# Gate and value products of four more chunks by seven block products, and attention blocks transposed in one instruction and moved by DMA

## The chip, the core and the metric

The kernel runs on one core of a Trainium2 chip. A core has five engines that run side by side, each through its own list of instructions in order: TensorE (PE; its weight loads are listed apart as PEld), VectorE (DVE), ScalarE (ACT), GpSimd (POOL) and SyncE (SP), which issues nearly all DMA transfers here. Engines wait for each other by semaphores. The metric is device time in microseconds (us).

## The reference

```python
# attention: batch 8, heads 8, seq 576, head_dim 64, fp32
scores = scale * np.matmul(q, k.transpose(0, 1, 3, 2))
mask_local = (rel >= 0) & (rel < stride)                       # stride 32, heads 0 to 3
mask_strided = (rel >= 0) & (pos[None, :] % stride == pos[:, None] % stride)   # heads 4 to 7
attn = softmax(where(mask, scores, -1e9)); attn_out = attn @ v
# gated feed-forward over x = attn_out as [4608 tokens, 512]
rms = np.sqrt(np.mean(x * x, axis=-1, keepdims=True) + 1e-06)
xn = x / rms * rms_g
g = xn @ w_gate                                                # 512 -> 1536
silu = g * (1.0 / (1.0 + np.exp(-g)))
val = xn @ w_val
return (silu * val @ w_out).astype(np.float32)                 # 1536 -> 512
```

Both masks are sparse: only the score blocks that a mask leaves are computed.

## The kernel before, in words

**Attention.** Work is cut into 96 units `(b, p, j)`: a batch, a pair of heads, a third of the rows. A unit has two heads and one or two blocks of up to 128 query rows. `step_s` does scores (TensorE into the bank `pair`), row minimum with the mask (VectorE, L624, into `pp`), exponentials (ScalarE, L632) and normalisation (POOL or VectorE, L641). `step_t` transposes the probabilities into `pT`: since VectorE transposes blocks of 32 by 32, it issues one instruction for each 32-row block on the diagonal and beside it (L684). `step_o` multiplies by V and writes the result into `raw`, one buffer for each chunk of 512 tokens, three in turn. Units from 28 on (`BT`) have scores two at a time and values four at a time.

**Feed-forward.** There are 9 chunks of 512 tokens. In chunks 0 to 6 (`NCL` = 7) a slot is one of 12 units `u` of 128 hidden columns: gate product, value product (`gemm1`), gating (L922, L924, L935), and the output product (`slot_o`) of the slot before. Every fp32 product is made of three fp32r ones (high x high, low x high, high x low), so gate and value take 4 x 3 matmuls of 512 columns each and the output product 12. Chunks 7 and 8 are computed as a pair (`pair_of_chunks`): as a 2 x 2 block product (two chunks and two halves of the 512 inputs, times two halves and gate/value), by Strassen's scheme with seven block products of 6 matmuls per unit instead of eight. It uses four transformed weight blocks per unit, made by `transform_gv` during that stage, and for the output product `transform_o`, made beside earlier chunks.

**Buffers.** Gate and value weights of all 12 units stay in SBUF (`wg0` to `wv11`), split into high and low. Output weights pass through a ring of five buffers `or0` to `or4`: each slot reloads one from the copy `wos` in DRAM as soon as the slot five earlier has used it (`stream`, L1630).

**Order.** All work is entered as operations with a duration and the buffers that they read and write. A planner (`Plan`) puts them in order, engine by engine, by due times that it works out backwards; its switches (`PASS_A`, `PASS_B`, `SWITCH`, `BA`, `BM`) decide what goes first. At run time each engine keeps to its list.

Of the kernel before, what the change touches and what calls it, by code (L numbers as in the profile page):

```python
# [10 lines left out]
F32 = mybir.dt.float32  # L11
# [12 lines left out]
P = 128  # L24
# [4 lines left out]
NCL = NCH - 2  # L29
NX = 3  # L30
# [7 lines left out]
NCST = 510  # L38
# [19 lines left out]
BA = 10000.0  # L58
BM = 20000.0
# [42 lines left out]
NPB = 4  # L102
# [242 lines left out]
def attn_moe(ctx: ExitStack, tc: tile.TileContext, qT: bass.AP, kT: bass.AP, vl: bass.AP, vs: bass.AP,  # L345
# [13 lines left out]
    cb = sbt([P, 382], "cb", BF16)  # L359
    mloc = cb[:LQ, 0:256].rearrange("p (t k) -> p t k", k=P)  # L360
    m7 = cb[:126, 256:382]
    m6 = cb[:108, 256:364]
# [36 lines left out]
    identb = sbt([P, 2 * CH], "hl0", BF16)[:, 0:P]  # L399
    stat = [[sbt([P, 2, 2], f"mx{i}") for i in range(4)], [sbt([P, 2, 2, 2], f"su{i}") for i in range(4)]]  # L400
# [38 lines left out]
    for x in range(6):  # L439
        op("Pool", 100, -1, lambda x=x: nc.gpsimd.memset(xx[x][:, 0:PAD], 0.0), writes=[("xp", x)])  # L440
    for x in range(NPB):
        op("Pool", 600, -1, lambda x=x: nc.gpsimd.memset(pbuf[x], 0.0), writes=[("pp", x)])

    for i in range(4):
        op("Pool", 70, -1, lambda i=i: nc.gpsimd.memset(stat[1][i][:, :, :, 1:2], 1e-9), writes=[("st", i)])

# [3 lines left out]
    wus = [(b, p, j) for b in range(NB) for p in ((2, 3, 0, 1) if b == NB - 1 else range(NH // 2)) for j in range(3)]  # L450
# [4 lines left out]
    starts, turns, outs = {}, {}, {}  # L455
    for i in range(n_pro - TLAG, last + 1):
        s = i - n_pro
        if i >= n_pro:
            starts.setdefault(s - (i >= BT and (i - BT) % 2), []).append(i)
        if i < PP0:  # L460
            turns[s + TLAG] = turns.get(s + TLAG, []) + [i]
            d = s + TLAG + (i >= GR0 and (i - GR0) % 2 == 0 and i + 1 < PP0)
            outs[d] = outs.get(d, []) + [i]
        else:
            turns[s + 1] = turns.get(s + 1, []) + [i]
            d = s + (PG - 1 - (i - PP0) % PG if i < last - 3 else (last - i) % 2) + PVL
            outs[d] = outs.get(d, []) + [i]
# [6 lines left out]
    def tb(i):  # L474

        return (i - PP0) % PG if i >= PP0 else i % (NTB - 1)
# [18 lines left out]
    wos = [dp.tile([P, 1024], F32, name=f"wos{u}") for u in range(NU)]  # L495
    for n, u in keys:
        wraw[n, u] = sb.tile([P, 1024], U32, name=f"w{n}{u}")
# [12 lines left out]
    def slot_of(o, x):  # L510
        return (2 * o + x) % 6

    def load(b, p, at):
# [24 lines left out]
        if o == 0:  # L538
            op("SP", 430, at + 2, lambda: nc.sync.dma_start(out=identb, in_=consts[:, 382:510]), writes=[("hl", 0)],
               bytes_=P * P * 2)  # L540
            op("SP", 430, at + 2, lambda: nc.sync.dma_start(out=cb, in_=consts[:, 0:382]), writes=["cb"],
               bytes_=P * 382 * 2)
# [158 lines left out]
    def step_o(units):  # L701

        reads, length, todo = [], 0.0, []
        for x, i in enumerate(units):
# [4 lines left out]
            reads += [tk, ("vt", (4 * b + p) % 2)]  # L709
            length += 2 * len(tl) * 0.84 * m if i >= n_pro else PF * 2 * len(tl) * 1.26 * m + 30  # L710
# [14 lines left out]
        for x, (i, vt, m, n, tl, pT, po) in enumerate(todo):  # L725
            b, p, j = wus[i]
            base, nt = S * b, len(tl)
            cs = set()
# [23 lines left out]

            def evac(e, moves=moves):
# [39 lines left out]
    def rms(c, bk, at):  # L793
        if c == 1:
            op("PE", 900, at, lambda: nc.tensor.matmul(out=bank[bk], lhsT=ones, rhs=ssq, start=True, stop=True),
               reads=["ones", "ssq"], writes=[bk])
        elif c:
# [10 lines left out]
            def lo(e):  # L808
                two["l"] = sb.tile([P, CH], F32R, name="pT2")
# [6 lines left out]
            def blank():  # L816
                tbufs[2] = sb.tile([P, CH], F32, name="pT2")
                nc.gpsimd.memset(tbufs[2], 0.0)
            op("ACT", act(CH), at, hi, reads=["ssq"], writes=["srt"], also=[("DVE", 345, True)])
            op("Pool", pool(CH), at, lo, reads=["ssq", "srt"], writes=[("pT", 2)], also=[("DVE", dve(CH), True)])  # L820
            op("PE", 470, at, total, reads=["onesr", "srt", ("pT", 2)], writes=[bk] + ([("S", 0), ("T", 0)] if bk[0] == "b" else []))
            if c < NCL:
                op("Pool", 600, at, blank, writes=[("pT", 2)])
# [37 lines left out]
    def convert(c, at, kcs=range(KC)):  # L861
        rt = raw[c % NX]
        for kc in kcs:
# [90 lines left out]
    def slot_o(c, u, at):  # L954
        h = 0
        if (c, u) in ((1, 0), (1, 10), (2, 2), (3, 4), (4, 6), (5, 8)):
            b = plan.boost
            plan.boost = 0.0
            transform_o(u // 2, c)
            plan.boost = b  # L960
        for t in (0, 2, 1, 3) if c < NCL - 1 else range(4):
# [6 lines left out]
            op("PE", 681, at + t, fn, reads=[("hh", h), ("hl", h), wkey(("o", u, c))], writes=[("S", t // 2 + 1), ("T", t // 2 + 1), f"a{t}"] if u == 0 and c == 0 else [f"a{t}"], chain=True)  # L968
        stream(c, u)
        if u == NU - 1:  # L970
            for t in (0, 2, 1, 3):
                k, ob = (("ssq", ssq), ("srt", None), (("pp", 0), pbuf[0]), (("pp", 1), pbuf[1]))[t % 2]

                def evac(e, t=t, ob=ob):
                    ob = roots["srt"] if ob is None else ob
# [41 lines left out]
    def last_root():  # L1017
# [17 lines left out]
        def hi(e):  # L1035
            two["h"] = sb.tile([P, CH], F32R, name="pp0")
# [5 lines left out]
        def lo(e):  # L1042
            two["l"] = sb.tile([P, CH], F32R, name="pp1")
# [5 lines left out]
        op("ACT", act(CH), 0, hi, reads=[k0], writes=[("pp", 0)], also=[("DVE", 345, True)])  # L1049
        elementwise(CH, lo, [k0, ("pp", 0)], [("pp", 1)])  # L1050
# [48 lines left out]

    def transform_gv(u, z=0):  # L1100
# [676 lines left out]
```

## Time and profile before

| | |
|---|---|
| median of 3 runs | 1019.2 us (1018.59 to 1023.23) |
| profiled execution | 1019.23 us, its span 1017.4 us |
| granted TensorE clock, mean | 0.992 |
| matmul instructions in the trace | 5356 |
| HBM read, written | 98.09 MB, 22.02 MB |

The span runs from the first to the last instruction; the profiled execution's own time has 1.8 us around it. In the trace, chunk 0 runs from about 55 to 175 us, the pair at the end from about 835 us. "Busy" is the time in which an engine had an instruction under way. "Idle before" is the time just before an instruction, with the one that ended the wait.

### The profile page before, as it was taken

What the parts mean: (1) busy time and instruction counts of PE and PEld (TensorE: products, weight loads), DVE (VectorE), ACT (ScalarE), POOL (GpSimd) and SP (SyncE); (2) the same over time, 40 slices, a digit from 0 to 9 for tenths busy, and PEclk for the clock granted to TensorE, in tenths of its full rate; (3) what the DMA queues carried; (4) which work ended last, traced back from release to release, by engine and by line L of the source; (5) the groups of instructions that cost most, each with busy time, mean ns of one, the idle gap of its engine ahead of it and who ended that gap; (6) DMA issues with size and microseconds to landing.
All of it is one profiled execution on the core that took longest, in us unless ns stands there. A gap on an engine that the chain in (4) does not pass through costs nothing.

```text
span 1017.4 us, 15890 instructions
## 1 busy us (share of the span) xinstructions
PE 999.3 (98%) x5356; PEld 803.9 (79%) x5356; DVE 690.5 (68%) x1985; ACT 484.7 (48%) x1357; POOL 420.9 (41%) x400
## 2 busy tenths in 40 slices
PE   8999998999999999999999999999999999999998
PEld 6777775787887888788888888788877778887886
DVE  4699999715767617762566436777666968778891
ACT  6899966413454325441454226441554434334450
POOL 6333368414573313642236313263224443767500
PEclk9799999999999999999999999999999999999999
DMA  9876434423353214332243323232322101120451
GB/s 308 294 268 221 163 132 144 156 64 102 135 191 114 95 62 149 121 120 72 86 142 119 115 85 128 91 112 102 103 83 79 42 0 42 42 83 1 156 166 72
DMA packets 52561, 121.14 MB, mean 119 GB/s; under 512 B 5312, under 2 KB 21248, under 8 KB 52480
## 3 DMA queue, kind: packets, MB, share of 16 engines
q1 hardware_dynamic: 51712, 119.28, 35.1%
q10 hardware_dynamic: 768, 0.85, 0.3%
q8 instruction: 42, 0.69, 0.3%
q14 instruction: 39, 0.32, 0.1%
HBM read 98.09 MB, written 22.02 MB: 118 GB/s over the span
## 4 chain that ended last, share of the span: by engine, by line
PE 90%; DVE 7%; issue 1%; ACT 1%; DMA 1%; DVEq 0%; ACTq 0%
PE g L909 22%; PE v L909 21%; PE acc L966 21%; PE pair L604 4%; PE g L1295 3%; PE pair L721 3%; PE v L1295 3%; PE pair L1295 3%; PE g L1460 2%; PE acc L1460 2%; PE v L1460 2%; PE acc L1295 1%; PE pair L1460 1%; DVE pT L684 1%; DMA xx<-in_qT_dram 1%
## 5 line engine op out<-in xcount | busy, mean ns | idle before, releaser
L951 POOL TENSOR_TENSOR hl<-e,hh 128x512 fp32r<-128x512 f32 x84 | 115.1, 1370 | 271.9 <-ACT hh L942 260.4
L909 PE MATMUL g<-xh,wg 128*128 128x512 f32 x672 | 212.7, 398 | 1.0 <-DVE e L924 0.7
L966 PE MATMUL acc<-or,hh 128*128 128x512 f32 x672 | 210.1, 394 | 0.7 <-POOL or L1607 0.7
L909 PE MATMUL v<-xh,wv 128*128 128x512 f32 x664 | 208.6, 395 | 1.2 <-DVE wv L1607 0.9
L924 DVE SCALAR_TENSOR_TENSOR e<-e,g 128x512 f32<-128x512 f32 x84 | 57.5, 685 | 145.3 <-ACT e L922 144.8
L966 PEld LDWEIGHTS acc<-or,hh 128*128 128x128 f32 x672 | 124.7, 188 | 28.6 <-POOL or L1607 1.0
L909 PEld LDWEIGHTS g<-xh,wg 128*128 128x128 f32 x672 | 123.1, 188 | 30.3 <-DVE e L924 2.4
L909 PEld LDWEIGHTS v<-xh,wv 128*128 128x128 f32 x664 | 122.8, 188 | 30.2 <-DVE wv L1607 1.3
L909 PE MATMUL g<-xl,wg 128*128 128x512 f32 x336 | 131.3, 391 | 2.0 <-DVE xl L885 2.0
L966 PE MATMUL acc<-or,hl 128*128 128x512 f32 x336 | 131.0, 390 | 0.1
L641 POOL TENSOR_TENSOR pp<-pp,mx 96x512 f32<-96x512 f32 (+3 forms) x87 | 84.2, 975 | 109.7 <-DVE mx L638 64.7
L909 PE MATMUL v<-xl,wv 128*128 128x512 f32 x332 | 129.4, 390 | 0.0
L632 ACT ACTIVATE pp<-pp,mx 96x128 f32<-96x128 f32 (+2 forms) x296 | 113.5, 386 | 20.4 <-DVE mx L624 20.1
L942 ACT CAST hh<-e 128x512 fp32r<-128x512 f32 x84 | 52.2, 622 | 145.7 <-PE acc L966 131.9
L684 DVE STREAM_TRANSPOSE pT<-pp 32x128 f32<-32x128 f32 (+1 forms) x376 | 109.6, 292 | 14.5 <-POOL pp L641 7.7
L922 ACT ACTIVATE e<-g 128x512 f32<-128x512 f32 x84 | 50.1, 597 | 139.8 <-PE g L909 131.2
L935 DVE SCALAR_TENSOR_TENSOR e<-e,v 128x512 f32<-128x512 f32 x83 | 57.0, 687 | 32.2 <-PE v L909 27.2
L909 PEld LDWEIGHTS g<-xl,wg 128*128 128x128 f32 x336 | 63.2, 188 | 16.0 <-DVE xl L885 2.4
L966 PEld LDWEIGHTS acc<-or,hl 128*128 128x128 f32 x336 | 63.1, 188 | 14.2 <-POOL hl L951 0.7
L909 PEld LDWEIGHTS v<-xl,wv 128*128 128x128 f32 x332 | 62.3, 188 | 13.4
L624 DVE CUSTOM_DVE_ANT_0 pp<-pair,cb 96x128 f32<-96x128 f32 (+2 forms) x296 | 65.6, 277 | 10.2 <-PE pair L604 8.3
L632 ACT ACTIVATION_READ_ACCUMULATOR pp<-pp,mx 96x1 f32 (+2 forms) x296 | 55.8, 188 | 0.0
(494 smaller groups left out, 1620.4 us busy)
## 6 DMA issues: line engine op xcount, KB each, us to landing
or<-wos SPq DMA_DIRECT2D x72, 512.0 KB, 3.3
xx<-in_qT_dram SPq DMA_DIRECT2D x31, 288.0 KB, 3.4
xx<-in_kT_dram SPq DMA_DIRECT2D x28, 288.0 KB, 3.0
wg<-in_wgv_dram SPq DMA_DIRECT2D x12, 512.0 KB, 8.7
vt<-in_vl_dram SPq DMA_DIRECT2D x16, 384.0 KB, 3.7
wv<-in_wgv_dram SPq DMA_DIRECT2D x12, 512.0 KB, 6.0
or<-in_wo_dram SPq DMA_DIRECT2D x12, 512.0 KB, 3.6
wos<-or SPq DMA_DIRECT2D x12, 512.0 KB, 5.0
```

Source lines behind the costliest of these rows:

```text
L624: nc.vector.tensor_tensor_reduce(out=pv[:, h, x], in0=sp[h][:, x], in1=mk[:, x], scale=-0.125, scalar=3.0e38, op0=ALU.add, op1=ALU.min, ac ...
L632: nc.scalar.activation(out=pv[:, h, x], in_=sp[h][:, x] if i < PM else pv[:, h, x], func=AF.Exp, scale=0.125 if i < PM else -1.0, bias=mx[ ...
L641: (nc.vector if e == "DVE" else nc.gpsimd).tensor_tensor(out=pv, in0=pv, in1=mx.unsqueeze(3).broadcast_to([m, 2, nt, n]), op=ALU.mult)
L684: nc.vector.transpose(out=dst[32 * y:32 * y + 32, :, 32 * x:32 * x + 32], in_=src[32 * x:32 * x + 32, :, 32 * y:32 * y + 32])
L909: nc.tensor.matmul(out=out, lhsT=wt[:, w, sl], rhs=xhl[x, kc], start=(kc == 0 and i == 0), stop=(kc == KC - 1 and i == 2))
L924: op("DVE", dve(CH), at + MO, lambda: nc.vector.scalar_tensor_tensor(out=e, in0=e, scalar=1.0, in1=bank["g"], op0=ALU.add, op1=ALU.mult), ...
L935: op("DVE", dve(CH), at + MO, lambda: nc.vector.scalar_tensor_tensor(out=e, in0=e, scalar=0.5, in1=bank_of(c, ("v", u))[0], op0=ALU.mult, ...
L942: nc.scalar.copy(out=hh[h], in_=e)
L951: (nc.vector if n == "DVE" or h else nc.gpsimd).tensor_tensor(out=hl[h], in0=e, in1=hh[h].bitcast(F32), op=ALU.subtract)
L966: nc.tensor.matmul(out=acc[t], lhsT=x[h][:, sl], rhs=wt[:, w], start=(u == 0 and i == 0), stop=(u == NU - 1 and i == 2))
L1295: nc.tensor.matmul(out=banks[bk], lhsT=w, rhs=X[a, k].tile(y), start=start and k == 0 and i == 0, stop=stop and k == 1 and i == 2, skip_gr ...
L1460: nc.tensor.matmul(out=banks[bks[j]], lhsT=tile(v, k, j), rhs=x.tile(y), start=start and k == 0 and i == 0, stop=stop and k == KT - 1 and ...
```

## The change

Chunks 3 to 6 are now computed in two pairs as well, (3,4) and (5,6), by `plain_pair`: gate and value of the 12 units by seven block products each, all 24 gated tiles kept, and then the 24 output products as before, 12 matmuls each. To make room, the pair's split inputs lie in the places of the weights of units 0 to 4, and gated tiles in places of weights already used. So all gate and value weights are also written to DRAM once (`wgs`), the transformed weights too (`tgv`, made beside chunks 1 and 2), and they are loaded again when they are needed (`load_t`, `load_moved`, `back`). Attention units are spread over the slots so that both chunks of a pair are ready when it begins.

For units from 28 on, two units share one buffer of 1024 columns, laid out so that one VectorE instruction transposes all 32 x 32 blocks in place (`step_d`). The seven blocks on and beside the diagonal are then moved to other partitions by seven DMA transfers of 32 KB.

Other edits: `xx` has five buffers instead of six, `pp` and `pT` two of double width; `pT2` is no longer used for sums of squares; the planner's switches have other values.

```diff
+NS1 = 3
+MS = 6
+S0 = 13
-BA = 10000.0
-BM = 20000.0
+BA = 0.0
+BM = 0.0
-PASS_A = ([25.0, 0.0, 150.0, 37.5], 0.3, 4000.0, 8)
-PASS_B = ([25.0, 900.0, 225.0, 300.0], 0.2, 4000.0, 7)
-SWITCH = 180000.0
+PASS_A = ([50.0, 50.0, 300.0, 300.0], 0.1, 4000.0, 7)
+PASS_B = ([12.5, 450.0, 600.0, 800.0], 0.4, 4000.0, 3)
+SWITCH = 120000.0
...
+    def step_d(i):
+        x, u = (i - BT) // 2 % 2, (i - BT) % 2
...
+        op("DVE", DVT + 2 * CH / 0.96, 0, lambda: nc.vector.transpose(out=pq[x], in_=pq[x]), reads=[], writes=[("pu", x, 0), ("pu", x, 1), ("pp", x)])
+        moves = [(y, z) for y in range(4) for z in (y, y + 1) if z < 4]
+        for k, (y, z) in enumerate(moves):
+            op("SP", 430, 0, lambda y=y, z=z: nc.sync.dma_start(out=DX[x][32 * z:32 * z + 32, y].rearrange("k g q -> k (g q)"),
+                                                                in_=PX[x][32 * y:32 * y + 32, z].rearrange("k g q -> k (g q)")),
+               reads=[("pp", x)], writes=[("pd", x, k)], bytes_=32 * 1024)
...
+    def load_t(u, i):
+        for w in range(2):
+            def fn(w=w):
+                TS[i, w] = sb.tile([P, 2 * CH], F32R, name=f"{'tl' if w else 'th'}{i}" if i < 2 else f"or{w}")
+                nc.sync.dma_start(out=TS[i, w].bitcast(F32), in_=tgv[u][:, 1024 * w:1024 * w + 1024])
...
+    def plain_pair(c, beside):
...
+        natural = [f"w{n}{u}" for u in range(5) for n in "gv"]
...
+            args = {"1": ("A11", p, basic("g", 0), gk, True, False), "5": ("S1", r, trans(1), tkw, True, False),
+                    "6": ("S2", p, trans(2), tkw, False, False), "2": ("A12", q_, basic("g", 256), gk, True, True),
+                    "3": ("S4", r, basic("v", 256), vk, False, True), "7": ("S3", p, trans(3), tkw, False, False),
+                    "4": ("A22", p, trans(4), tkw, False, True)}
...
+        for u in range(RING):
+            ring_load(("o", u, c), every(wtag(("o", u, c)))[1:])
+        for tag in natural + ["wv8", "wv10"]:
+            back(tag)
...
+        for s in range(2):
+            for u in range(NU):
...
+                slot_o(c + s, u, 0, z, True)
...
+                if s == 1:
+                    back(hslot[u])
...
+        if n != "o":
+            op("SP", 430, at, lambda: nc.sync.dma_start(out=wgs[n, u], in_=W[key].rearrange("p w n -> p (w n)").bitcast(F32)),
+               reads=[wk], writes=[("wgs", key)], bytes_=P * 4096)
...
+    for c in range(NS1, NCL, 2):
+        plain_pair(c, beside)
     pair_of_chunks(NCL)
```

The change moves instructions at three places that matter below.

**TensorE, gate and value in chunk 3.** Before, unit 8: each row multiplies one of four input blocks (`xh` high, `xl` low) by the unit's gate (`wg8`) or value weights (`wv8`), into the bank `g` or `v`; x2 stands for two matmuls.

```order
L909 MATMUL g_68<-xh2_574,wg8_1324 128x512 x2
L909 MATMUL g_68<-xl2_579,wg8_1324 128x512
L909 MATMUL v_69<-xh2_574,wv8_1375 128x512 x2
L909 MATMUL v_69<-xl2_579,wv8_1375 128x512
L909 MATMUL g_68<-xh3_634,wg8_1324 128x512 x2
L909 MATMUL g_68<-xl3_666,wg8_1324 128x512
L909 MATMUL v_69<-xh3_634,wv8_1375 128x512 x2
L909 MATMUL v_69<-xl3_666,wv8_1375 128x512
```

Now one block product is six matmuls; the split inputs lie under the names of weights (`wg3`, `wv3`), the weights are transformed ones (`th0`, `tl0`) or reloaded ones (`wv7`, `wv8`), and the products go into four banks.

```order
L1820 MATMUL g_68<-wv3_3976,th0_4645 128x512
L1820 MATMUL acc01_70<-wg1_3449,wv7_4341 128x512 x3
L1820 MATMUL acc01_70<-wv1_3447,wv7_4341 128x512 x3
L1820 MATMUL acc23_71<-wg4_4053,wv8_4401 128x512 x3
L1820 MATMUL acc23_71<-wv4_4040,wv8_4401 128x512 x3
L1820 MATMUL g_68<-xh0_4020,th0_4645 128x512
```

The banks `acc01` and `acc23`, which the output product of the slot before filled between these rows, belong to gate and value here; the output products stand behind all twelve units.

**SyncE, reloads.** Before, in a chunk of the loop, output weights (`or` from `wos`) come one for each slot, among inputs of attention (`xx`, `vt`), transformed weights on their way out (`to`) and results.

```order
L1630 DMA or0_3655<-wos4_118 128x1024
L985 DMA out_0_dram<-srt_3490 128x512
L985 DMA out_0_dram<-ssq_100 128x512
L1630 DMA or1_3734<-wos5_119 128x1024
L554 DMA vt0_82<-in_vs_dram 126x2x320
L536 DMA xx0_76<-in_qT_dram 128x576
L536 DMA xx1_77<-in_kT_dram 128x576
L1630 DMA or2_3865<-wos6_120 128x1024
```

Now, where the output products of the pair (5,6) begin, gate and value weights (from `wsg`, `wsv`) stand between them; all but the `vt` row are 512 KB.

```order
L1925 DMA wg3_6811<-wsg3_132 128x1024
L1925 DMA wv2_6813<-wsv2_131 128x1024
L2085 DMA or0_6822<-wos5_119 128x1024
L1925 DMA wv3_6825<-wsv3_133 128x1024
L583 DMA vt1_82<-in_vl_dram 128x768
L1925 DMA wg4_6838<-wsg4_134 128x1024
L1925 DMA wv4_6841<-wsv4_135 128x1024
L1925 DMA wv10_6846<-wsv10_147 128x1024
L2085 DMA or1_6855<-wos6_120 128x1024
L2085 DMA or2_6871<-wos7_121 128x1024
```

The weight of slot 6 (`wos6`) moved behind four weights of the next stage in SyncE's queue.

**VectorE and SyncE, the transposes.** Before, VectorE's list beside a late chunk has the block transposes of two units as seven instructions each (x4 and x3, for the two halves of a unit's blocks).

```order
L935 SCALAR_TENSOR_TENSOR e_99<-e_99,v_69 128x512
L684 STREAM_TRANSPOSE pT1_97<-pp1_93 32x4x32 x4
L684 STREAM_TRANSPOSE pT0_96<-pp0_92 32x4x32 x3
L684 STREAM_TRANSPOSE pT1_97<-pp1_93 32x4x32 x3
L810 TENSOR_TENSOR pT2_6014<-ssq_100,srt_6002 128x512
```

Now VectorE has one row for two units, `STREAM_TRANSPOSE pp1_92<-pp1_92 128x1024`, and SyncE seven moves behind it; here with what each waits for (DMAHW0 to 7 are eight counters that transfers take in turn, so a wait on one is for the transfer eight places earlier).

```order
L1226 DMA tg6_156<-th0_2004 128x1024 [waits DMAHW4_49,Activation_49]
L1226 DMA tg6_156<-tl0_2058 128x1024 [waits DMAHW5_49,DVE_49]
L663 DMA pT1_94<-pp1_92 32x256 [waits DMAHW6_49,DVE_49]
L663 DMA pT1_94<-pp1_92 32x256 [waits DMAHW7_49]
L663 DMA pT1_94<-pp1_92 32x256 [waits DMAHW0_49]
L663 DMA pT1_94<-pp1_92 32x256 [waits DMAHW1_49]
L663 DMA pT1_94<-pp1_92 32x256 [waits DMAHW2_49]
L663 DMA pT1_94<-pp1_92 32x256 [waits DMAHW3_49]
L663 DMA pT1_94<-pp1_92 32x256 [waits DMAHW4_49]
L2085 DMA or4_3250<-wos5_119 128x1024 [waits DMAHW5_49,DVE_49,PE_49]
```

The values product of TensorE waits for the last of the moves instead of the last block transpose.

More of the change, by code (lines that the diff above doesn't have):

```diff
@@ L455, in attn_moe @@
     starts, turns, outs = {}, {}, {}
+    where = {}
+    for i in range(n_pro - TLAG, BT):
+        where[i] = i - n_pro
+    i0, s0 = BT, S0
+    for c in range(NS1, NCL + 1, 2):
+        i1 = min(12 * (c + 2), last + 1)
+        for i in range(i0, i1):
+            where[i] = s0 + int((i - (i - BT) % 2 - i0) * (NU * c - (MS if c < NCL else MSL) - s0) / (i1 - i0))
+        i0, s0 = i1, NU * c + 1
     for i in range(n_pro - TLAG, last + 1):
-        s = i - n_pro
+        s = where[i]
         if i >= n_pro:
-            starts.setdefault(s - (i >= BT and (i - BT) % 2), []).append(i)
+            starts.setdefault(s, []).append(i)
         if i < PP0:
@@ L474, in tb @@
     def tb(i):
-        return (i - PP0) % PG if i >= PP0 else i % (NTB - 1)
+        return (i - BT) // 2 % 2 if i >= BT else i % (NTB - 1)
     def tkey(i):
@@ L495, in attn_moe @@
     wos = [dp.tile([P, 1024], F32, name=f"wos{u}") for u in range(NU)]
+    wgs = {(n, u): dp.tile([P, 1024], F32, name=f"ws{n}{u}") for n, u in keys}
+    tgv = [dp.tile([P, 2048], F32, name=f"tg{u}") for u in range(NU)]
+    done_x, done_u = set(), set()
     for n, u in keys:
@@ L510, in slot_of @@
     def slot_of(o, x):
-        return (2 * o + x) % 6
+        return (2 * o + x) % (5 if o < XO else 4)
     def load(b, p, at):
@@ L751, in step_o @@
                     i1 = i2
+            assert all(c < NX or c - NX in done_x for c in cs), (i, cs)
             def evac(e, moves=moves):
@@ L793, in rms @@
     def rms(c, bk, at):
+        busy.discard(c)
+        rooted.add(c)
+        assert not flight or c < 2
+        assert all(i in done_u for i in range(12 * (c + 1) - 4 * (c == NB - 1))), c
         if c == 1:
@@ L952, in slot_h, with slot_o @@
         op("Pool", pool(CH), at + MO, lo, reads=[ek, ("hh", h)], writes=[("hl", h)] + more, also=way("f", ("DVE", dve(CH), True)))
[L954 to L961, printed above, removed]
+    def slot_o(c, u, at, h=0, far=False):
+        first = c >= NS1 and (c - NS1) % 2 == 0 and u == 0
+        for t in (0, 2, 1, 3):
             def fn(t=t):
@@ L1365, in quad @@
             return step, after
-        transform_gv(2, 0)
+        for u in range(NS):
+            load_t(u, u)
         steps = [quad(u) for u in range(NU)]
@@ new lines, in scores_of @@
+    def scores_of(units):
+        for i in units:
+            b, p, j = wus[i]
+            if j == 0:
+                load(b, p, 0)
+                if i < PP0:
+                    load_v(b, p, 0)
+        if units[0] >= BT:
+            todo = [step_e(i) for i in units]
+            op("PE", SC0 + sum(x[2] for x in todo), 0, lambda: [x[0]() for x in todo], reads=[y for x in todo for y in x[1]],
+               writes=[("S", 0), ("T", 0)], lock=("b0", "b1"))
+            for x in todo:
+                x[3]()
+            return
+        for i in units:
+            step_s(i)
@@ new lines, in values_of, with before @@
+    def values_of(units):
+        step_o(units)
+        for i in units:
+            b, p, j = wus[i]
+            if j == (2 if b < NB - 1 or p > 1 else 0):
+                square(b, p, 0)
+            n = turn.index((b, p)) + 2
+            if j == 2 and i + 4 >= PP0 and n < len(turn):
+                load_v(*turn[n], 0)
+    def before(s):
+        plan.boost = BA if s >= NU * CB else 0.0
+        for i in turns.get(s, []):
+            if i < PP0:
+                step_t(i)
+        if s in starts:
+            scores_of(starts[s])
@@ new lines, in behind, with roots_of, beside @@
+    def behind(s):
+        plan.boost = BA if s >= NU * CB else 0.0
+        if s in outs:
+            values_of(outs[s])
+        for i in turns.get(s, []):
+            if i >= PP0:
+                step_t(i)
+    def roots_of(s, bk="g"):
+        for c in range(1, NB - 1):
+            if not flight and c not in rooted and all(i in done_u for i in range(12 * (c + 1))):
+                rms(c, bk, 0)
+    def beside(s):
+        before(s)
+        behind(s)
+    tslots = {TV0 + k * (NU * NS1 - 2 - TV0) // NU: k for k in range(NU)}
@@ L1681, in attn_moe @@
+    for c in range(NS1):
+        more = c + 1 < NS1
+        for u in range(NU):
+            at, s = T(c, u), NU * c + u
+            before(s)
             plan.boost = BM if c >= CB else 0.0
@@ L1685, in attn_moe @@
                 convert(c + 1, at + CVO)
-            plan.boost = BA if c >= CB else 0.0
-            if pvs:
-                values_of(pvs)
-            for i in turn:
-                if i >= PP0:
-                    step_t(i)
+            now = u == 0 and c > 0 and not flight
+            if now:
+                plan.boost = BM if c >= CB else 0.0
+                slot_o(c - 1, NU - 1, at + SOO)
+            behind(s)
             plan.boost = BM if c >= CB else 0.0
```

556 lines of the change are left out of this document (436 added, 120 removed), and 2 rows, old and new, of the table xplace.

## The prediction

> **What bounds the kernel now.** I read the page first: the busy line, the chain of work that ended last, the rows on DMA. The first says who is busy, the second who is late, the third what is left of a resource that the change uses more.
>
> ```profile
> PE 999.3 (98%) x5356; PEld 803.9 (79%) x5356; DVE 690.5 (68%) x1985; ACT 484.7 (48%) x1357; POOL 420.9 (41%) x400
> ...
> DMA  9876434423353214332243323232322101120451
> GB/s 308 294 268 221 163 132 144 156 64 102 135 191 114 95 62 149 121 120 72 86 142 119 115 85 128 91 112 102 103 83 79 42 0 42 42 83 1 156 166 72
> ...
> q1 hardware_dynamic: 51712, 119.28, 35.1%
> ...
> PE 90%; DVE 7%; issue 1%; ACT 1%; DMA 1%; DVEq 0%; ACTq 0%
> ```
>
> TensorE is busy for 98% of the span and holds 90% of the chain. So a matmul that goes is worth its own time, as long as nothing else becomes late. DMA is used to 35%: 119.28 MB took 35.1% of 16 engines over 1017.4 us, which makes 334 GB/s at full use; the busiest slice reached 308.
>
> Then I asked for busy times by stage: PE, PEld, DVE, ACT, POOL, granted clock, DMA share and GB/s in each stretch.
>
> ```profile
> 55.00:175.00 120.00, 114.29 (x640) 87.53 (x640) 113.63 (x291) 99.80 (x248) 60.01 (x47) 1.00 0.53 182
> 175.00:295.00 120.00, 119.99 (x636) 96.88 (x637) 70.94 (x261) 51.04 (x151) 53.83 (x51) 1.00 0.37 123
> ...
> 835.00:960.00 125.00, 123.22 (x543) 101.53 (x542) 101.12 (x138) 51.94 (x90) 76.92 (x64) 1.00 0.19 60
> ...
> 800.00:825.00 25.00, 24.16 (x105) 19.03 (x103) 20.18 (x23) 8.48 (x14) 15.51 (x10) 1.00 0.07 22
> 850.00:875.00 25.00, 25.00 (x112) 20.69 (x111) 20.01 (x28) 9.61 (x17) 14.20 (x13) 1.00 0.01 3
> 925.00:950.00 25.00, 23.21 (x103) 18.86 (x102) 21.66 (x27) 9.82 (x17) 16.30 (x13) 1.00 0.09 27
> ```
>
> Chunk 1 on (175 us) leaves TensorE without a gap and VectorE 59% busy. Chunk 0 (55 to 175 us) is the warning: with VectorE at 113.63 of 120 us, TensorE lost 5.71 us. In the pair at the end (835 to 960 us), VectorE at 101.12 of 125 cost TensorE 1.78 us.
>
> **The change part by part.** All of it is set against the profiled execution, 1019.23 us (span 1017.4 and 1.8 around it), which equals the median of the runs shown, 1019.2.
>
> *Fewer products.* A pair of chunks needs 12 x 2 x 24 = 576 matmuls of 512 columns for gate and value; by seven block products it needs 12 x 7 x 6 = 504. Two pairs save 144. At 25.00/112 = 0.223 us (row of 850 us) that is **-32.1 us**, all on the path.
>
> *Wider attention blocks.* Score blocks of 108 columns become 128, and so do the transposed ones.
>
> ```profile
> L604 PE MATMUL pair<-xx,xx 64*108 64x108 f32 x168 | 13.0, 271 | 0.0
> ...
> L604 PE MATMUL pair<-xx,xx 64*126 64x126 f32 x112 | 9.4, 285 | 0.0
> ...
> L721 PE MATMUL pair<-pT,vt 108*64 108x108 f32 x108 | 8.0, 263 | 0.2 <-DVE pT L684 0.2
> ```
>
> The program has 72 such score and 72 such value matmuls after unit 28; the trace records each as two. 13.0/168 = 77 ns against 9.4/112 = 84 ns: 7 ns for 18 columns more, 144 records, 1 us, and less for the values. In proportion to the columns (18%) it would be 2 us each. I take **+2 us** (1 to 4).
>
> *Transposes.* 444 block transposes go; 34 instructions of 1024 columns come.
>
> ```profile
> L684 DVE STREAM_TRANSPOSE pT<-pp 32x128 f32<-32x128 f32 x320 | 96.4, 301 | 13.2 <-POOL pp L641 7.2 <-PE pair L721 1.6
> ...
> L684 DVE STREAM_TRANSPOSE pT<-pp 32x64 f32<-32x64 f32 x56 | 13.2, 236 | 1.3 <-POOL pp L641 0.5
> ```
>
> 64 columns more cost 65 ns, so 1024 columns are about 1.2 us: 41 us for what took some 130. This relief lies off the path, so I count it only in VectorE's load below.
>
> *VectorE in chunks 1 and 2.* Here the change piles work up: the attention of chunks up to 4 must be ready when chunk 3 begins, so 120 row minima instead of 72 run beside these slots, and all twelve gate/value transforms with six output transforms. From the second chunk's first gating multiply to the third chunk's last the order gives VectorE:
>
> ```profile
> L624 DVE CUSTOM_DVE_ANT_0 pp<-pair,cb 96x128 f32<-96x128 f32 x156 | 35.3, 281 | 0.7 <-POOL pp L641 0.4
> ...
> L924 DVE SCALAR_TENSOR_TENSOR e<-e,g 128x512 f32<-128x512 f32 x84 | 57.5, 685 | 145.3 <-ACT e L922 144.8
> ...
> L853 DVE RECIPROCAL srt<-srt 128x128 f32<-128x128 f32 x28 | 24.1, 911 | 0.0
> ...
> L1094 DVE TENSOR_TENSOR tl<-tt,th 128x512 fp32r<-128x512 f32 x9 | 9.6, 1066 | 0.3
> ...
> L1015 DVE TENSOR_TENSOR tt<-tt 128x256 f32<-128x256 f32 x13 | 7.1, 572 | 0.3
> ...
> L1011 DVE TENSOR_TENSOR tt<-wv 128x512 f32<-128x512 f32 x6 | 6.3, 1050 | 0.0
> ...
> L1011 DVE TENSOR_TENSOR tt<-wg 128x512 f32<-128x512 f32 x4 | 2.7, 681 | 0.0
> ```
>
> 120 row minima at 35.3/156 = 0.226 (27 us), 16 large transposes (19), 46 gating multiplies at 0.685 (32), 12 reciprocals and 12 scalings at about 0.91 (22), 19 sums at 0.68 to 1.05 (13 to 20), 43 half differences at 0.572 (25), 29 low parts at 0.68 to 1.07 (20 to 31), and some 42 us of copies, casts, reductions and small sums: **200 to 218 us**. TensorE has 23 slots x 36 x 0.223 = 185 us there and some 30 of attention, 215 us. So VectorE stands at 93% or more, as in chunk 0, where TensorE lost 5.71 of 120. In proportion that is 10 us; where the short durations hold, 2 us as in the pair stage. I take **+7 us** (-2, since chunk 0 itself loses six transposes, to +34).
>
> *DMA in the output stages.* Per pair, gate and value use up the buffers in which weights stood. So 24 output products of 12 x 0.223 = 2.68 us each follow one another, and beside them the weights come back. Program order from the first reload of the second pair's end to its last output weight has 46 transfers of 512 KB, and with outputs and moves 26.5 MB; in the first pair 23.3 MB. TensorE's counted work from their first chance to the last need is about 76 and 74 us. At 334 GB/s the transfers take 79 and 70 us. The tight place is slot 6 of the second: 10.8 MB are queued ahead of its weight and its two neighbours, 32 us at 334, with about 26 to spare. I take **+6 us** (0, if the first are issued early enough, to 12 at 308).
>
> [...] The trace here never shows more than 308 in a slice.
>
> *Block moves.* Seven transfers of 32 KB follow each transpose.
>
> ```profile
> SPq L1567 <- DMA wos<-or: 19.5, 7, 3.9
> ...
> 39.17 0.33 SPq L551 DMA_DIRECT2D vt<-in_vl_dram  x1
> ...
> wg<-in_kT_dram ACTq DMA_DIRECT2D x1, 48.0 KB, 2.3
> or<-wos SPq DMA_DIRECT2D x72, 512.0 KB, 3.3
> ...
> L632 ACT ACTIVATE pp<-pp,mx 96x128 f32<-96x128 f32 x156 | 60.6, 391 | 8.7 <-DVE mx L624 8.6
> ...
> L632 ACT ACTIVATION_READ_ACCUMULATOR pp<-pp,mx 96x1 f32 x156 | 29.4, 188 | 0.0
> ...
> L641 POOL TENSOR_TENSOR pp<-pp,mx 96x512 f32<-96x512 f32 x42 | 45.9, 1100 | 55.7 <-DVE mx L638 50.4 <-DVE mx L637 2.7 <-DVE v L830 2.4
> ```
>
> An issue holds SyncE's queue 0.33 us or more, a landing takes 2.3 to 3.3: 5 to 6 us from the transpose to the values, where a transposed block was usable at once. Also each issue waits until the eighth transfer before it has landed (the order shows the counters; the first row above is such waits). The cover: row minima 2, exponentials 8 x (60.6 + 29.4)/156 = 4.6, normalisation 1 to 2, transpose 1.2 and moves 5 to 6 make 14 to 16 us after a pair's scores, and TensorE's order puts 16.6 to 45 us of its own work between the second scores of a group and its values. Behind a late values product stand the gate products of the next slot. Four of the 17 groups have under 18 us. I take **+2 us** (0 to 34).
>
> *Epilogues beside attention.* The seven-product stage ran without attention so far and lost 1.78 of 125 us; now ScalarE's blocks of exponentials (half of those 4.6 us a unit) stand between its copies. Two such stages: **+3 us** (0 to 10). In return the gaps of the last pair, 0.84 and 1.79 us at 800 and 925 us, end beside transforms that are done by then: **-2 us**.
>
> Sum: -32.1 + 2 + 7 + 6 + 2 + 3 - 2 = **-14 us, 1005 us**.
>
> **The rivals.**
>
> *Nothing is late.* For it: TensorE stood 0.01 us in 120 from 175 us on, though seven chunks of dependent work ran beside it. Against it: the 5.71 us of chunk 0 at the same load of VectorE. 1019.2 - 32.1 + 2 + 1 = 990 us.
>
> *DMA becomes the bound of the output stages.* All traffic grows from 119 to 220 MB. At the 308 GB/s of the busiest slice the second stage stalls 12 us, the first 4, and reloads run over into the next gate products: some 16 instead of 6, 1015 us. For it: 26.5 MB in 76 us is 349 GB/s. Against: the rate of 334 is measured over small transfers too.
>
> *VectorE takes TensorE's place in chunks 1 and 2.* This one ends slower. The forecast gains 21 us without its +7, so it decides from the point where VectorE needs 236 us there, 224 us of work at 95%. The longest rows show how:
>
> ```profile
> L1094 DVE TENSOR_TENSOR or<-xx,or 128x512 fp32r<-128x512 f32 x2 | 3.4, 1718 | 0.0
> ...
> L885 DVE TENSOR_TENSOR xl<-raw,xh 128x512 fp32r<-128x512 f32 x17 | 15.1, 891 | 0.0
> ```
>
> With 29 low parts at 1.72 and the sums at 1.05 it is 237 us, at 95% use 249, 34 us over TensorE's 215: 1032 us. Against it: 1.72 is a mean of two.
>
> *The moves come late.* If each of the 17 groups holds TensorE 2 us, that is 34 instead of 2: 1037 us; from 1 us a group the gain is gone. For it: a move stands behind 512 KB transfers in one queue. Against: the slack above.
>
> [...]
>
> That the change doesn't do what it says is left at 1 in 50: the order counts 144 matmuls fewer.
>
> **How the numbers follow.** The forecast (997 to 1013) gets 0.42, nothing late 0.17, DMA 0.15, VectorE 0.13, late moves 0.10, the rest 0.03. The likeliest gives 1005 us. The range 989 to 1026 leaves out most of the two slow cases and little below. A measurement of this kernel can tell about 0.5%, 5 us. Faster (under 1014): forecast, nothing late, two thirds of DMA: 0.68. Within 0.5%: the rest of DMA and the mild ends of the slow cases, 0.14. Slower: 0.18.
>
> **What would show it.** Right: about 3650 matmuls of 512 columns at 0.22 us; PE gaps in chunks 1 and 2 of some 7 us with VectorE over 90%; gaps in the output stages released by a DMA into the output weights' ring; large transposes of about 1.2 us. Wrong: PE waits on the moves' landing summing to over 10 us, output stages without gaps at over 330 GB/s, or VectorE under 85% in chunks 1 and 2 with gaps nonetheless.

## The result and the profile after

| | before | after |
|---|---|---|
| median (range) | 1019.25 us (1018.59 to 1023.23, 4 runs) | 1030.42 us (1029.04 to 1033.63, 4 runs) |
| profiled execution, its span | 1019.23 us, 1017.4 us | 1029.79 us, 1026.9 us |
| granted TensorE clock, mean | 0.992 | 0.988 |
| matmul instructions in the trace | 5356 | 5212 |

The ratio is 1.0106, 95% interval 1.0071 to 1.0141: the changed kernel is slower by about 11 us, where 14 less were forecast.

The page of the changed kernel, with the lines that answer to those of before (busy time by engine, DMA share and GB/s in 40 slices, the queue that carries nearly all transfers, the chain that ended last):

```profile
PE 987.6 (96%) x5212; PEld 780.4 (76%) x5212; DVE 743.1 (72%) x1749; ACT 501.5 (49%) x1394; POOL 302.1 (29%) x286
...
DMA  9999654456467476355666869554679793462551
GB/s 301 314 377 354 220 207 167 145 192 226 157 210 273 138 235 227 122 168 199 198 204 211 292 231 369 204 199 162 192 235 355 241 391 117 151 205 82 155 174 61
...
q1 hardware_dynamic: 88768, 220.43, 62.8%
...
PE 76%; DVE 10%; DMA 8%; SPq 2%; ACT 2%; issue 1%; POOL 0%; ACTq 0%; DVEq 0%
```

144 matmuls are gone, but TensorE's busy time fell by 11.7 us (999.3 to 987.6), not by 32. And its idle time rose from 18.1 to 39.3 us (span less busy). These are two separate losses. The chain shows the second: DVE, DMA and SP's queue hold 20% of it now.

Where the idle time lies is told by busy times in stretches (columns as before: PE, PEld, DVE, ACT, POOL, granted clock, DMA share, GB/s):

```profile
55.00:175.00 120.00, 113.41 (x607) 85.99 (x607) 112.83 (x269) 96.10 (x241) 45.98 (x38) 0.99 0.74 274
175.00:295.00 120.00, 113.84 (x663) 88.13 (x664) 100.00 (x286) 61.96 (x207) 70.58 (x62) 1.00 0.52 171
295.00:400.00 105.00, 94.21 (x579) 74.11 (x577) 85.22 (x223) 54.30 (x168) 63.15 (x55) 0.97 0.66 220
...
325.00:350.00 25.00, 18.78 (x109) 15.13 (x109) 20.80 (x62) 13.94 (x43) 16.33 (x15) 0.86 0.46 143
...
825.00:850.00 25.00, 24.65 (x118) 19.63 (x115) 22.10 (x37) 6.27 (x13) 0.00 (x0) 1.00 1.02 403
...
875.00:900.00 25.00, 25.00 (x110) 20.34 (x110) 12.12 (x19) 7.52 (x13) 0.00 (x0) 1.00 0.41 137
```

In chunks 1 and 2 (175 to 400 us) TensorE idles 225 - 208.05 = 17 us, in stretches that had no gap before. VectorE is not full there: 100.00 of 120 and 85.22 of 105 us, 83 and 81%. The row of 875 us shows the first loss: TensorE without a gap, products of 512 columns only, 110 in 25 us where before had 112.

Groups of instructions (busy, mean ns of one, idle before and its releasers):

```profile
L616 DVE CUSTOM_DVE_ANT_0 pp<-pair,cb 96x128 f32<-96x128 f32 (+2 forms) x248 | 55.5, 283 | 27.9 <-DMA pT<-pp 15.8 <-PE pair L610 8.6 <-PE acc L1088 2.9
L660 DVE STREAM_TRANSPOSE pp<-pp 128x1024 f32<-128x1024 f32 x34 | 42.1, 1237 | 9.1 <-POOL pp L646 8.9
```

VectorE's row minima (L616) waited 15.8 us for the block moves. One such place, in order of time (start, duration, engine, line, operation; idle before in brackets):

```profile
319.22 2.12 SPq L583 DMA_DIRECT2D vt<-in_vl_dram  x2
...
319.34 1.22 DVE L660 STREAM_TRANSPOSE pp<-pp 128x1024 f32<-128x1024 f32 x1
...
321.44 4.36 SPq L663 DMA_DIRECT2D pT<-pp  x7
...
327.83 0.29 DVE L616 CUSTOM_DVE_ANT_0 pp<-pair,cb 96x128 f32<-96x128 f32 x1 [0.93 <-DMA pT<-pp]
...
329.65 0.58 PE L610 MATMUL pair<-xx,xx 64*126 64x128 f32 x2 [4.57 <-DVE my L616]
```

The transpose ends at 320.56. SP is still issuing two other loads, then the seven moves, 0.62 us each, until 325.80; the last lands about 2 us later. Only then may a row minimum write into that buffer again, and VectorE keeps to its order. The next scores wait for those row minima to empty the bank `pair`: TensorE stands for 4.57 us. The granted clock of 325 to 350 us, 0.86, shows what came with this gap: half the clock from 327.4 to 334.2 us, and so for 4.5 us after TensorE had begun again at 329.65. In this trace shorter gaps were followed by it, too: after 2.46 us at 149 us and after 2.29 us at 782 us the clock was halved for 3.4 us each, while in run e9 (below) one of 2.5 us before 175 us passed without (granted clock 1.00 over 55 to 175 us, 0.99 here).

An account of the 9.5 us between the two spans: 144 products fewer at 227.6 ns, -32.8; idle time, +21.2; clock not granted (1.2% of 1026.9 against 0.8% of 1017.4 us), +4; slower products, +12.7 (next section); wider blocks +2; some 2 us remain unexplained.

### The profile page after: what moved, and what is told of

Read it like the earlier page. It is cut to its first block, busy times and chain, and to the rows that moved or that the text cites. A ratio compares the mean times of both kernels' runs of the same rounds, so it can differ in the third digit from the quotient of the medians.

```text
span 1026.9 us, 16263 instructions
## 1 busy us (share of the span) xinstructions
PE 987.6 (96%) x5212; PEld 780.4 (76%) x5212; DVE 743.1 (72%) x1749; ACT 501.5 (49%) x1394; POOL 302.1 (29%) x286
## 4 chain that ended last, share of the span: by engine, by line
PE 76%; DVE 10%; DMA 8%; SPq 2%; ACT 2%; issue 1%; POOL 0%; ACTq 0%; DVEq 0%
PE acc L1088 18%; PE acc L1820 9%; PE g L1036 7%; PE g L1820 6%; PE v L1036 6%; PE v L1820 6%; PE v L1449 3%; PE pair L1449 3%; PE g L1449 3%; DMA or<-wos 2%; PE pair L610 2%; PE pair L832 2%; SPq L663 2%; DMA pT<-pp 2%; PE v L1615 2%; PE g L1615 2%
## 5 line engine op out<-in xcount | busy, mean ns | idle before, releaser
L646 POOL TENSOR_TENSOR pp<-pp,my 96x512 f32<-96x512 f32 (+2 forms) x68 | 68.8, 1029 | 165.2 <-DVE my L639 51.1
L623 ACT ACTIVATE pp<-pp,my 96x128 f32<-96x128 f32 (+2 forms) x248 | 96.2, 390 | 39.5 <-DVE my L616 27.6
L1036 PE MATMUL g<-xh,wg 128*128 128x512 f32 x288 | 93.9, 407 | 0.3 <-DVE e L1051 0.2
L1036 PE MATMUL v<-xh,wv 128*128 128x512 f32 x280 | 91.1, 406 | 2.7 <-DVE e L1062 2.1
L616 DVE CUSTOM_DVE_ANT_0 pp<-pair,cb 96x128 f32<-96x128 f32 (+2 forms) x248 | 55.5, 283 | 27.9 <-DMA pT<-pp 15.8
L1078 POOL TENSOR_TENSOR hl<-e,hh 128x512 fp32r<-128x512 f32 x36 | 51.1, 1420 | 74.4 <-ACT hh L1069 73.0
L1036 PEld LDWEIGHTS v<-xh,wv 128*128 128x128 f32 x280 | 52.0, 190 | 17.2 <-DVE e L1062 3.1
L1088 PE MATMUL acc<-or,xh 128*128 128x512 f32 x192 | 61.8, 403 | 2.3 <-DMA or<-wos 2.3
L1036 PEld LDWEIGHTS g<-xh,wg 128*128 128x128 f32 x288 | 51.5, 189 | 14.6 <-DVE e L1051 1.4
L1036 PE MATMUL g<-xl,wg 128*128 128x512 f32 x144 | 57.0, 396 | 0.6 <-DVE xl L1012 0.6
L1036 PE MATMUL v<-xl,wv 128*128 128x512 f32 x140 | 55.5, 396 | 0.0
L1088 PEld LDWEIGHTS acc<-or,hl 128*128 128x128 f32 x240 | 45.2, 188 | 10.8
L660 DVE STREAM_TRANSPOSE pp<-pp 128x1024 f32<-128x1024 f32 x34 | 42.1, 1237 | 9.1 <-POOL pp L646 8.9
```

The source lines that it names most:

```text
L616: nc.vector.tensor_tensor_reduce(out=PX[x][:m, :, g0 + 2 * h + t], in0=sp[h][:, t], in1=mk[t], scale=-0.125, scalar=3.0e38, op0=ALU.add, o ...
L623: nc.scalar.activation(out=v, in_=v, func=AF.Exp, scale=-1.0, bias=mx2[x][:m, u, h, t:t + 1], accum_out=su2_[x][:m, u, h, t, 0:1])
L646: (nc.vector if e == "DVE" else nc.gpsimd).tensor_tensor(out=v, in0=v, in1=s.unsqueeze(1).unsqueeze(3).broadcast_to([m_, 4, 2 * n_, 32]), ...
L660: op("DVE", DVT + 2 * CH / 0.96, 0, lambda: nc.vector.transpose(out=pq[x], in_=pq[x]), reads=[], writes=[("pu", x, 0), ("pu", x, 1), ("pp" ...
L1036: nc.tensor.matmul(out=out, lhsT=wt[:, w, sl], rhs=xhl[x, kc], start=(kc == 0 and i == 0), stop=(kc == KC - 1 and i == 2))
L1078: (nc.vector if n == "DVE" or h else nc.gpsimd).tensor_tensor(out=hl[h], in0=e, in1=hh[h].bitcast(F32), op=ALU.subtract)
```

## The experiments

"Pitch" is the distance from the start of one 512-column matmul to that of the next, as the mean over neighbours at most 260 ns apart. It is worked out from all start times of a trace: 227.6 ns before, 231.1 ns after. 3.5 ns on 3656 products are the 12.7 us above. It is a mean over all products, and products that the change left alone are slower, too, as one group of the last pair shows, first before, then after:

```profile
L1295 PE MATMUL g<-raw,wg 128*128 128x512 f32 x36 | 9.1, 389 | 0.0
```

```profile
L1449 PE MATMUL g<-raw,wg 128*128 128x512 f32 x36 | 9.3, 394 | 0.0
```

**Alignment to 64 bytes (refuted).** The five `xx` rows of 628 floats (576 + 32 + 20; the expectation below says 660) put nearly every tile behind them 32 bytes off a multiple of 64; before, all stood on multiples.

```diff
-    xx = [sbt([P, SW + 20], f"xx{i}") for i in range(5)]
+    xx = [sbt([P, SW + 32], f"xx{i}") for i in range(5)]
```

> The changed kernel with its five xx rows 660 -> 640 floats long (SW + 20 -> SW + 32), so that every tile behind them starts at a multiple of 64 bytes, as in the kernel before; the program is the same instruction by instruction. Theory A (rows that start 32 bytes off a multiple of 64 slow every product): pitch of the 512-column products falls from 231.1 ns to before's 227.6, 3653 x 3.5 ns = 13 us: 1017 to 1018, TensorE busy about 975. Rival (the slower pace comes from the chip's clock or from the transfers, 220 MB): pitch stays at 231, 1029 to 1031.

Measured (e1): 1029.28 us (ratio to before 1.0080, 1.0060 to 1.0099), pitch 231.4 ns. The converse, in the kernel before:

```diff
+    sbt([P, 8], "shift")
     raw = [sbt([P, KC, CH], f"raw{i}") for i in range(NX)]
```

> The kernel before with one tile of 8 floats ahead of raw, which puts every tile behind it 32 bytes off a multiple of 64; nothing else. Theory A: pitch 231 instead of 227.6, 3797 x 3.5 ns = 13 us: 1031 to 1033. Rival: no change, 1019.

Measured (e2): 1019.17 us (0.9996, 0.9980 to 1.0013), pitch 227.6 ns. Both say no: where the tiles move together, nothing happens.

**The block moves (theory B).** Both kernels have e1's rows, so e1 is their baseline.

```diff
-            op("SP", 430, 0, lambda y=y, z=z: nc.sync.dma_start(
+            op("SP", 430, 0, lambda y=y, z=z, k=k: (nc.scalar if k % 2 else nc.sync).dma_start(
```

> e1's kernel with three of the seven block moves of each pair issued by ACT's queue instead of SP's; the order on the other engines stays. Theory B (the seven moves, issued one behind another in 4.4 us and landing 2 us later, hold the pair's tile, so VectorE's row minima two pairs on wait for them, 15.8 us in all, and TensorE behind them): the moves land 1.8 us earlier, VectorE's waits for pT<-pp fall below 8 us, TensorE's gaps in 175 to 400 us fall from 17 to about 9: 7 us below e1. Rival (VectorE's load itself makes these gaps): within 2 us of e1. Other rival (ACT is held by the moves' waits): ACT's exponentials come later, 3 to 10 us above e1.

Measured (e3): 1021.85 us (1.0018, 1.0000 to 1.0036), 7.4 below e1. What VectorE's row minima waited for, by releaser (us, times):

```profile
its engine sat idle before it (us, times) until:
  PE pair L610: 7.4, 8
  DMA pT<-pp: 5.1, 5
```

The wait for moves fell from 17.1 us in e1 to 5.1. TensorE's gaps in 175 to 400 us fell less, from 13.9 us to 10.8, where 9 had been expected. Over the whole span TensorE idles 3.8 us less than in e1; the rest of the gain is busy time (992.2 to 988.6 us), at a mean granted clock of 0.987 against 0.983. Then no moves at all:

```diff
-        op("DVE", DVT + 2 * CH / 0.96, 0, lambda: nc.vector.transpose(out=pq[x], in_=pq[x]), ...)
-        for k, (y, z) in enumerate(moves):
-            op("SP", 430, 0, lambda y=y, z=z: nc.sync.dma_start(...), ...)
+        def blocks():
+            for y, z in moves:
+                nc.vector.transpose(out=DX[x][32 * z:32 * z + 32, y].rearrange("k g q -> k (g q)"),
+                                    in_=PX[x][32 * y:32 * y + 32, z].rearrange("k g q -> k (g q)"))
+        op("DVE", 7 * (DVT + 256 / 0.96), 0, blocks, reads=[], writes=[("pu", x, 0), ("pu", x, 1), ("pp", x)] + [("pd", x, k) for k in range(7)])
```

> e1's kernel without block moves: per pair seven 32x256 VectorE transposes straight into place instead of one 128x1024 and seven transfers. VectorE gets about 7 x 0.43 - 1.24 = 1.8 us more per pair, 17 x 1.8 = 31 us, two thirds of it in 175 to 400 us, where it is busy 185 of 225 us. Theory B: no wait for moves is left and there is still room on VectorE: TensorE's gaps in 175 to 400 us fall below 8 us, time 5 to 10 us below e1. Rival (VectorE's load makes the gaps): the gaps grow to 25 to 40 us, 8 to 20 us above e1.

Measured (e4): 1017.76 us (0.9976, 0.9961 to 0.9991), 11.5 below e1. Its stretches of chunks 1 and 2:

```profile
175.00:295.00 120.00, 120.00 (x707) 94.39 (x705) 105.48 (x347) 67.98 (x227) 78.00 (x72) 1.00 0.55 186
295.00:400.00 105.00, 100.89 (x602) 78.98 (x601) 95.04 (x253) 53.39 (x160) 70.44 (x61) 0.98 0.56 193
```

VectorE works more here (200.5 of 225 us, against 185.5 in e1) and TensorE's gaps shrink to 4.1 us, from 13.9 in e1; what is left waits for ScalarE (2.7 and 1.4 us). So VectorE's load did not make the gaps. That its waits for the moves made them rests on e3 as well, since e4 changes more than the moves: the planner orders every engine anew, and some 40 other instructions of VectorE go to ScalarE and GpSimd. The block transposes take 61 us more than the large ones (1.8 for each of 34 pairs, where the expectation had counted 17), but VectorE's busy time grows by 33 us only. e3 leaves the order of all other work as it was.

**Doubling the suspected wait.** This run has the placement of e9 (below), its baseline.

```diff
+            def move(y=y, z=z):
+                for g in (0, 4):
+                    nc.sync.dma_start(out=DX[x][32 * z:32 * z + 32, y, g:g + 4].rearrange("k g q -> k (g q)"),
+                                      in_=PX[x][32 * y:32 * y + 32, z, g:g + 4].rearrange("k g q -> k (g q)"))
```

> e9's kernel with each block move issued as two of half the columns: 14 transfers per pair from SP's queue instead of seven, the same bytes. Theory B: the last lands some 4 us later per pair, VectorE's wait for pT<-pp grows from 15 to 35 to 60 us over 16 close pairs, and the time by 8 to 25 us over e9. Rival (what counts is only the 2 us to land, or VectorE's load): within 3 us of e9.

Measured (e12): 1130.17 us (1.1088, 1.1053 to 1.1123), 111.5 above e9. The wait grew as expected, the time far more. The page's busy line, then a wait of VectorE and one of TensorE (total, times, longest), then SP's queue at one place:

```profile
PE 1011.7 (90%) x5212; PEld 803.0 (71%) x5212; DVE 735.7 (65%) x1749; ACT 500.7 (44%) x1394; POOL 300.3 (27%) x286
```

```profile
DVE pp L616 <- DMA pT<-pp: 60.4, 13, 8.0
...
PE pair L834 <- DMA pT<-pp: 20.4, 8, 7.8
```

```profile
329.75 9.73 SPq L665 DMA_DIRECT2D pT<-pp  x14
```

The wait went from 15.8 us in e9 to 60.4, the top of what was expected. But fourteen moves hold SP's queue for 9.7 us instead of 4.7 (medians of the 34 pairs), and what stands behind them there comes late too; TensorE also waits for the moves directly. It idles 114 us (e9: 41). Its mean granted clock fell to 0.950 (e9: 0.990), and the same instructions keep it busy 37.6 us longer (974.1 to 1011.7). The expectation had left out the queue and the clock. So e12 shows that the moves are dear, but not how much of the 111.5 us is VectorE's wait alone.

**Distance between two sets of tiles (theory C).** e1 and e2 moved all tiles behind `xx` alike. What differs between the kernels is a distance. Between `hl0` and `tt` lie the small statistics tiles: 256 bytes a partition before, 448 after, with `my0`, `my1`, `sv0`, `sv1` (192 bytes) among them. All large tiles ahead of that gap (`xh` to `hl0`) hold multiples of 2048 bytes, and those behind (`tt`, `th`, `tl`, `wg`, `wv`, `or`) multiples of 4096. So a product of one set with the other has its streamed rows and its weights 256 bytes apart (mod 512) before, 448 after. Products of two tiles behind the gap stand a multiple of 512 apart in both, and the changed kernel's own trace tells them apart: neighbours that take `wv` with `wv` have a pitch of 228.6 ns, those that take `or` with `hh`, one from each side, 233.0. In e9 (below), where 448 is 256 again, both are near 228 (227.8 and 228.5).

```diff
-    mx2 = [sbt([P, 2, 2, 2], f"my{i}") for i in range(2)]
-    su2_ = [sbt([P, 2, 2, 2, 2], f"sv{i}") for i in range(2)]
...
+    mx2 = [sbt([P, 2, 2, 2], f"my{i}") for i in range(2)]
+    su2_ = [sbt([P, 2, 2, 2, 2], f"sv{i}") for i in range(2)]
     raw = [sbt([P, KC, CH], f"raw{i}") for i in range(NX)]
```

> The changed kernel with its four new small tiles (my0, my1, sv0, sv1: 192 bytes a partition) allocated ahead of raw instead of between hl0 and tt; instructions and order are unchanged. Rows of wg, wv, or, tt, th, tl then start 256 bytes (mod 512) from those of the x, hh, hl tiles, as in the kernel before, instead of 448. Theory C (a product is slower where the rows that it streams and the weights loaded beside it start 64 or 192 bytes apart, mod 256; in the traces so far the pitch is 228.4 ns at 0 and 230.8 to 233.2 elsewhere): pitch 231.1 -> 227.6 ns, 3653 x 3.5 ns = 13 us: 1016 to 1019. Rival (the pace belongs to the new order of products, or to the transfers): pitch 231, 1029 to 1031.

Measured (e5): 1024.94 us (1.0048, 1.0020 to 1.0076), pitch 228.2 ns. The pitch answered, the time only by half. Some products are still slow: those that stream `raw` or `xx` with `wg` have 233.0 and 234.1 ns here, 226.6 and 226.5 in e9, since with rows of 628 floats these tiles stand at distances that are not 0 mod 256. That and the profiled execution's granted clock (0.983 against 0.988) account for a part; the rest is open. The converse in the kernel before:

```diff
+    sbt([P, 48], "gap")
     xhl = {}
```

> The kernel before with one tile of 48 floats (192 bytes) between the small statistics tiles and tt; nothing else. Theory C: the two sets of tiles stand 448 bytes (mod 512) apart as in the changed kernel: pitch 231 to 233 instead of 227.6, 3797 products x 3.5 to 5.5 ns: 1032 to 1039. Rival: no change, 1019.

Measured (e6): 1033.28 us (1.0126, 1.0076 to 1.0177), pitch 231.3 ns. This is a program that does nothing new, with the price expected. In chunk 1, where TensorE has no gap, it gets through 625 matmuls in 120 us, before through 636:

```profile
175.00:295.00 120.00, 120.00 (x625) 95.71 (x626) 68.63 (x245) 49.10 (x145) 53.42 (x50) 0.99 0.34 115
```

e1's and e5's edits together restore every operand's place:

> The changed kernel with both of e1's and e5's edits: rows of 640 floats and the four small tiles ahead of raw, so that every operand stands as in the kernel before; the block moves are as the change has them. e5 left some tiles 32 bytes off and had a mean pitch of 228.2 ns and four more half-clock stretches than before. Theory C: pitch 227.6; with theory B the waits for the moves stay (15 us of VectorE's), so 1029 - 13 = 1016 to 1019. Rival (faster products run into the moves, so that half is given back): 1021 to 1025.

Measured (e9): 1018.63 us (0.9996, 0.9978 to 1.0014), pitch 227.6 ns. The group of the last pair is back at 389 ns:

```profile
L1449 PE MATMUL g<-raw,wg 128*128 128x512 f32 x36 | 9.1, 389 | 0.0
```

So placement cost the change 11.8 us, and the rival (half is given back to the moves) falls. Two gaps more in the kernel before, with `sbt([P, 16], "gap")` and `sbt([P, 32], "gap")`, ask which distances are dear:

> The kernel before with a gap of 64 bytes ahead of tt (e6 had 192): the two sets of tiles stand 320 bytes apart, 64 mod 128. If the pitch hangs on the distance mod 128: 231 to 232 ns, 1032 to 1036. If 192 is special (mod 256): up to 1025.

> The same with a gap of 128 bytes: the sets stand 384 bytes apart, 0 mod 128 and 128 mod 256. If the pitch hangs on the distance mod 128: 227.6 ns, 1019. If on the distance mod 256: 231 to 233 ns, 1032 to 1039.

Measured: 1036.28 us (e10; 1.0154, 1.0127 to 1.0180), pitch 232.4 ns; and 1032.77 us (e11; 1.0119, 1.0086 to 1.0152), pitch 232.0 ns. So 64, 128 and 192 (mod 256) are all dear, and 0 is cheap; that it goes by the distance mod 128 is refuted.

**Both together.** e3 and e4 with the small tiles ahead of `raw`:

> e3's kernel (moves from two queues) with the four small tiles ahead of raw as in e5. Theories B and C add up: 1022 - 13 = 1008 to 1010. Rival: 1021 to 1023. If the faster products make the moves late again, in between with longer waits of VectorE for pT<-pp (5.1 us in e3).

> e4's kernel (block transposes, no moves) with the four small tiles ahead of raw as in e5. If theories B and C both hold they add up: 1018 - 13 = 1004 to 1006, pitch 227.6, TensorE's gaps as in e4. Rival: nothing from the placement, 1017 to 1019.

Measured: 1008.60 us (e8; 0.9886, 0.9836 to 0.9936) with moves from two queues, and 1005.17 us (e7; 0.9851, 0.9805 to 0.9896) with block transposes: the two terms add up, and e7 beats both kernels. Its busy line:

```profile
PE 972.7 (97%) x5212; PEld 779.4 (78%) x5212; DVE 770.3 (77%) x1912; ACT 507.8 (51%) x1410; POOL 324.8 (32%) x309
```

## Why the prediction was wrong, point by point

**Fewer products, -32.1: the count was right, a term was missing.** 144 matmuls went, worth 32.8 us by the pitch (the 112 of a 25 us row include those that its edges cut). But the step priced the remaining ones at the pace of before. Four small tiles in the wrong place made 3656 products 3.5 ns slower on the mean: 12.7 us by the pitch, 11.8 us by e9 against the changed kernel. Nothing in the profile of before showed this, and no rival held it; the prediction read no addresses, and the section on the change does not list these tiles among its edits.

**Block moves, +2 (0 to 34): the term was mis-sized, since the wait was looked for in the wrong place.** e9 against e7 makes it 13.5 us, e1 against e4 11.5. The chain from scores to values was worked out well (TensorE waited for a landing 0.3 us in all). But two pairs of units share the buffers, so VectorE's row minima two pairs on need the moves landed as well, and behind a row minimum stand all of VectorE's work and, over the bank `pair`, the next scores. The rival "the moves come late" had the right transfers, but priced them too high (2 us for each of 17 groups of two pairs, an estimate that no run shows, against 13.5/17 = 0.8 measured), and named TensorE's values product in place of VectorE's order. That its 1037 us came near the measured time is luck: the placement, which it did not hold, made up the rest. Twice as many transfers of half the size cost 111 us more (e12 against e9).

**VectorE in chunks 1 and 2, +7, and the rival at 1032: refuted.** The load was put at 93% or more; it was 83 and 81%, with gaps nonetheless, which the prediction had named as a sign that it was wrong. e4 and e7 load VectorE more in these chunks (200.5 and 198.5 us against 185.2), and TensorE stands less (4.1 and 4.5 us against 17).

**DMA in the output stages, +6 (0 to 12): near, from a wrong rate.** The step took 334 GB/s as the most. The row of 825 us moved 403. TensorE waited for output weights 2.5 us:

```profile
PE acc L1088 <- DMA or<-wos: 2.5, 2, 2.3
```

**Wider blocks, +2, and large transposes, 1.2 us: right.** Score blocks that grew from 108 columns took 12.4/144 = 86 ns instead of 77; the transpose took 1237 ns.

**Epilogues beside attention, +3, and the last pair's gaps, -2: not tested apart.** In e9 TensorE idles 1.1 us between 400 and 700 us and 4.0 us between 700 and 1000, with 2.9 us for output weights among them, so neither can be large.

With the two terms put right, the prediction's own sum reads -14 + 12 + 11 = +9 us, or 1028; measured were 1030.4. That this comes so near is partly luck, since it keeps the +7 and the +6 and has no term for the clock. e7, without moves and with the placement of before, shows what the rest is made of. Its span is 14.4 us shorter than before: -32.8 for the products, +2 for the wider blocks, about +4 for the clock (0.988 against 0.992) and +12.2 of idle time (30.3 us against 18.1). Of that idle time 4.5 us lie in chunks 1 and 2, 4.0 ahead of them and 3.3 between 400 and 700 us; they have many releasers, and no run separates them. So e7 lands on the forecast of 1005 us with gaps of about the size forecast, but not for the reasons given. It is also another kernel: it pays for its transposes with 61 us more of VectorE's time (34 large ones took 42.1 us, 238 small ones 103.4 us), off the path.

## What to carry to other kernels

A transfer that replaces an instruction must be followed to everyone who needs its buffers, not just to who reads its result: here the reader had slack, and the next writer, on another engine's ordered list, had none. When a change adds even a small tile, compare where the operands of the hot loop stand relative to each other before and after; and check the time of one untouched instruction in both traces before explaining the rest. When a large gain on paper disappears, split the loss first into busy time that did not fall and idle time that grew: here the two had separate causes, and about half of the new idle time stayed when the moves were gone (18.1 us before, 41.2 in e9, 30.3 in e7).

## What the runs showed of the hardware

**In these runs a matmul's pace hung on the distance between its operands in SBUF.** With the two sets of tiles 0 mod 256 bytes apart, the pitch of 512-column fp32r products was 227.6 ns (before, e2, e7, e8, e9); at 64, 192 and 128 bytes 232.4, 231.3 and 232.0 (e10, e6, e11). That is 2%, 13 to 17 us of this kernel (1032.8 to 1036.3 against about 1019; TensorE busy 1016.4, 1012.3 and 1013.5 us against 999.3). Moving both by 32 bytes changed nothing (e2: 227.6 ns, 1019.17 us). Why the hardware does so is not shown.

**Small transfers held the queue that issued them.** A move's issue took 0.59 us of SP's queue (median), at 32 KB in the changed kernel and at 16 KB in e12 alike: half the size, and no less time. A load of 512 KB from `wos` took 0.33. And no transfer was issued before the last one on the same of the eight counters had landed: in the changed kernel's trace all 726 such issues came after that landing, 89 of them by less than 0.5 us.

**One idle gap cost more than its length.** With the 4.57 us gap of TensorE in the changed kernel came half the clock, until 4.5 us after the gap's end (0.86 on the mean of 325 to 350 us). In e12, where TensorE idled 114 us, the granted clock was 0.950 over the whole, with TensorE busy 37.6 us longer than in e9 (0.990, 41 us idle). What length of gap lowers the clock is not shown.
